# Two heads per transposing instruction and per set-aside copy in an attention and expert kernel, the last pair moved by copies, and a new order

## The chip, the cores and the metric

One core of one Trainium2 chip runs the whole program. The metric is device microseconds (us) of one execution; a time is the median of several. The core has five engines that this text calls by short names: PE (TensorE, matmuls), DVE (VectorE), ACT (ScalarE), POOL (GpSimd) and SP (SyncE, which here only issues DMAs). Each engine works through its own list of instructions in the order in which the program wrote them, and stops at an instruction whose inputs are not there yet.

## The reference

```python
q, k, v: (8, 8, 576, 64) float32            # batch, heads, sequence, head size
q_rot, k_rot = rotate(q), rotate(k)         # x1*cos - x2*sin, x1*sin + x2*cos
scores = matmul(q_rot, k_rot^T) / 8         # then minus the row maximum
attn = exp(scores) / (sum(exp(scores)) + 1e-9)
x = matmul(attn, v)                         # back to (8, 576, 512): heads side by side
for b in range(8):                          # routing and experts, one batch at a time
    score = x[b] @ w_gate
    top = the 128 tokens with the largest score
    y = relu(x[b, top] @ w1) @ w2           # w1 512x1024, w2 1024x512
    out[b] = x[b];  out[b, top] += sigmoid(score[top])[:, None] * y
```

## The kernel before, in words

Two heads of one batch make a pair; there are 32 pairs, four to a batch (`n_pairs`, `NP`). A pair goes through these steps, written by the functions named.

- `load` brings the pair's k, q and v from HBM. There is one buffer each for k and q (`k_in`, `q_in`), two for v (`vt`); half of v is copied once more to the other half of the partitions (L476, ACT or POOL).
- `rotate` makes the rotated k and q in two parts each, high and low, so that three matmuls of reduced precision give a float32 product. For every pair but the first this is POOL work: a product with the tables of cosines (L504), a sum (L510, and L514 for the last 64 places of q), and the difference from the rounded value (L520). ACT does the rounding (L519). For the first pair DVE does POOL's part, in pieces.
- `attend` does nine units of 128 rows: units 0 to 7 are four blocks of 128 positions for two heads, unit 8 holds the last 64 positions of both heads. `units` writes the matmuls of a unit, or of the two heads' units of a block together (L570: the groups qh kh, qh kl, ql kh). `softmax` then has DVE take the row minimum of the negated scores into SBUF (L591) and ACT the exponential and its sum (L599), into `pab` (two buffers, each with room for both heads of a block) or `pr` (unit 8).
- `turn` transposes a unit's 128x576 probabilities in 32x32 blocks by one DVE instruction (L622) into the tile `pt` and sets one half of the result aside by a copy of 128x288 (L628, ACT or POOL). `move` then exchanges halves between groups of 32 partitions by four DMAs on SP's queue (L654): two out of place, then two from the set-aside copy, which wait for the first two. This happens twice per pair: side 0 (`c` = 0) has units 0 to 3, side 1 has units 4, 5, 8, 6 and 7. For side 1 of the last pair the exchange is done by copies of 32x288 instead (L639, ACT or POOL), four per unit.
- `value` multiplies the transposed probabilities with v (L681, 36 instructions for a side, 72 passes in the trace), `rows_out` turns the result back (L734) and scales it by the reciprocal sums (L749 on ACT or L753 on DVE) into the rows of x; `half_done` stores them.
- After the fourth pair of a batch, `route` finds the 128 largest scores, `chosen` computes their indices (L896 is its last matmul), gathers those rows from HBM by an indirect DMA that POOL issues (L912), and `experts_of` transposes them (L930), does the two matrix products (L958, 192 instructions of the first and of the second each, over the eight batches) and scatters the result (L997, another indirect DMA of POOL). The tile `xe` is one buffer: a gather waits for the scatter of the batch before. The expert weights are loaded, rounded (L1022, ACT) and their low parts made (L1024, POOL, 16 instructions) beside the first pairs.

The order of all this is not the order in which it is written. Every step is entered with `op(engines, fn, key, after, ...)`: the engines that may do it with an assumed time for each, a due time `key` and the steps it must follow. `Order.run` then plays a small planner: at each moment it gives each free engine the waiting step with the smallest due time, whose inputs are ready by the assumed times, and where a step may go to one of two engines it goes to the one free first. The due times come from the dictionary `KEY` and a small random shift per pair drawn from `SEEDS`. When PE would be idle the planner adds a matmul that nobody reads (L367), if PE's recent busy share in its model is below `KEY["warm"]`. What is sent to the chip is then the list of instructions per engine in that order, with semaphores where one instruction reads or overwrites the data of another. The list `after` itself is read by the planner alone:

```python
o = op({"DVE": (675, 760)}, turns, key, exps[u] + area[c].before)
...
for _, _, o, e in order.run():
    o.fn(e) if len(o.engines) > 1 else o.fn()
```

Of the kernel before, what the change touches and what calls it, by code (L numbers as in the profile page):

```python
# [23 lines left out]
KEY = dict(warm=0.86, warm0=20000, warm1=1000000, dummy=430, dcols=256, ahead=15000, lag=16000, rem=400, value=17500, rows=5250, load=30500, rotate=173549, half=2500,
           gate=10237, route=21900, count=23781, select=5425, turn=24609, step=11400, count_=24062, select_=3000, turn_=98437, step_=10820, last_step=4750, kstep=2700, hold=3,
           vcopy=6000, lift=range(9), lifted=688, patience=900, over=450, near=-900, swap=9750, vsplit=9, vstep=2250, recip=7500, pool_lo=1, esplit=1, t_most=4, ring="SP", vring="SP", wring="SP", issue=250, svc0=800, svc1=200, svck=2101, svcq=2251, svcv=1501, first_moves=True, over_dma=750, patience_dma=1150)


SEEDS = (65, 53, 848, 188, 64, 106, 182, 56, 412, 765, 334, 840, 49, 811, 920, 630, 707, 350, 158, 580, 649, 829, 598,
         159, 606, 89, 919, 466, 149, 808, 916, 981, 466)  # L30
# [14 lines left out]
class Order:  # L45
# [4 lines left out]
    SEM = 45.0  # L50
    BLOCK, FETCH = 256, 3900.0
    WINDOW, FALL, RISE = 3413.0, 0.58, 0.88
    LANDED, FLYING = 500.0, 8


    TURN = {(a, b): t for t, froms, tos in (
# [222 lines left out]
def attention_moe_kernel(ctx: ExitStack, tc: tile.TileContext, q, k, v, gate, w1, w2, rope, outs, shape, cap):  # L279
# [51 lines left out]
    def act(n, more=0.0):  # L331
        return (65 + 0.833 * n + more, 165 + 0.833 * n + more)
# [120 lines left out]
    def at(pi, part):  # L453
        return PAIR * (pi + part)
# [34 lines left out]
    def rotate(pi):  # L489

        uses, got = loaded[pi]
        first = pi == 0
        key, base = at(pi, 0) - KEY["rotate"], at(pi, 0) - KEY["ahead"]
        if first:
            key = base = at(pi, 0) - 100000
        kh, kl, qh, ql = (r.next() for r in (khs, kls, qhs, qls))
        wait = list(last_first) if pi == 1 else []
        e = nc.vector if first else nc.gpsimd
        time = (lambda n: {"DVE": dve(n)}) if first else (lambda n: {"POOL": pool(n)})
        parts = {}  # L500

        def part(use, sum_use, sum_, tab, hu, lu, c0, c1, got, more=0):
            x, n = use.tile, c1 - c0
            m = op(time(2 * n), lambda: e.tensor_tensor(  # L504
                x[:, :, c0:c1], x[:, :, c0:c1], tab[:, :, c0:c1], op=ALU.mult), key + more, got)
            edge = name == "q" and c1 == S

            def add():
                m1 = MAIN if edge else c1
                e.tensor_tensor(sum_[:, c0:m1], x[:, 0, c0:m1], x[:, 1, c0:m1], op=ALU.add)  # L510
                for h in range(2) if edge else ():
                    hp = slice(64 * h, 64 * h + 64)
                    a, b = (x[hp, i, MAIN:S].rearrange("p (a j) -> p a j", j=32) for i in range(2))
                    e.tensor_tensor(striped(sum_)[hp, :, h], a, b, op=ALU.add)  # L514

            y = op(time(n) if not edge else {"DVE": dve(n, 1, 200.0)} if first else {"POOL": pool(MAIN, 540.0)}, add, key + more, [m] + sum_use.before)
            d1 = KW if edge else c1
            n = d1 - c0
            c = op({"ACT": act(n)}, lambda: nc.scalar.copy(hu.tile[:, c0:d1], sum_[:, c0:d1]), base + more, [y] + hu.before)  # L519
            d = op(time(n), lambda: e.tensor_tensor(  # L520
                lu.tile[:, c0:d1], sum_[:, c0:d1], hu.tile[:, c0:d1].bitcast(F32), op=ALU.subtract), base + more + 3000 * first, [c] + lu.before)
            use.by(m, y), sum_use.by(y, c, d), hu.by(c, d), lu.by(d)
            if first:
                last_first.append(y)
# [21 lines left out]
    def attend(pi):  # L546
# [61 lines left out]
        ready = lambda c: pts[c][:, area[c].tile:area[c].tile + 2 * (4 + c) * L]  # L608
        apart = lambda c: pts[c][:, side_[c].tile:side_[c].tile + (4 + c) * L]

        def turn(u, key):

            c = 1 if u == 8 else u // 4
            src, to = (pr.tile, 2) if u == 8 else (pab[u // 2].tile[:, u % 2 * S:u % 2 * S + S], (2 + c) * (u % 2) + u // 2 % 2)
            one = ready(c)[:, (1 + c) * to * L:(1 + c) * to * L + L]
            away = L if c else 4 * L
            two = bass.AP(tensor=one.tensor, offset=one.offset + away, ap=one.ap)

            def turns():
                into = one.rearrange("p (m o j) -> p m o j", o=1, j=32)  # L620
                into = bass.AP(tensor=into.tensor, offset=into.offset, ap=[*into.ap[:2], [away, 2], [1, 32]])
                nc.vector.transpose(into, src.rearrange("p (m w j) -> p m w j", w=2, j=32))  # L622

            o = op({"DVE": (675, 760)}, turns, key, exps[u] + area[c].before)
            (pr if u == 8 else pab[u // 2]).by(o)
# [8 lines left out]
            for g in (0, 2):
                e, o_ = slice(32 * g, 32 * g + 32), slice(32 * g + 32, 32 * g + 64)
                needs = [o, y]
                for out, in_ in ((two[e], one[o_]), (one[o_], apart(c)[e, to * L:to * L + L])):
                    needs = [op({"ACT": act(L, 30), "POOL": pool_copy(L)},
                                lambda e, out=out, in_=in_: (nc.gpsimd.tensor_copy if e == "POOL" else nc.scalar.copy)(out, in_),  # L639
                                key, needs)]  # L640
                    area[c].by(*needs), side_[c].by(*needs), moved[c].extend(needs)
# [510 lines left out]
```

## Time and profile before

| what | value |
| --- | --- |
| median of 3 runs | 584.03 us (583.14 to 585.76) |
| the profiled execution, its own time | 578.55 us |
| its span, first to last instruction | 576.5 us |
| PE busy, of which matmuls that nobody reads (L367) | 534.2 us, 51.9 us |
| DVE, ACT, POOL busy | 494.2, 478.2, 452.1 us |
| moved by DMA | 108.67 MB, mean 189 GB/s |
[...]

The profile is one execution, taken by the hardware profiler. Busy times are of the engine named; matmuls overlap, and their ends are modelled, so a busy PE is not PE at its peak. A row of instructions gives busy time, mean duration of one in ns, and how long the engine stood idle just before and what ended that. Durations of neighbours overlap at their ends: the spacing from start to start is shorter than a duration, and it is read from rows that merge several instructions.

### The profile page before, as it was taken

To read this page: it belongs to the slowest core of one execution; us is meant where nothing else is said; L and a number is where in the kernel's file an instruction comes from. 1 tells how busy PE (TensorE), PEld (TensorE's weight loads), DVE (VectorE), ACT (ScalarE), POOL (GpSimd) and SP (SyncE) were. 2 spreads that over 40 slices of the span, in tenths; PEclk is the share of its full clock that TensorE was granted. 3 is DMA by queue.
4 is the path that set the end of the run, shared out by engine and by line. 5 is a ranking of instruction groups with operands and counts; after the bars stand their busy time and mean duration, and the time that the engine had idled before them with its cause. 6 is when DMAs were issued, how large, how long until landed. Compare 5 with 4: busy or idle time off the path is not lost.

```text
span 576.5 us, 19632 instructions
## 1 busy us (share of the span) xinstructions
PE 534.2 (93%) x7558; PEld 443.7 (77%) x7558; DVE 494.2 (86%) x1249; ACT 478.2 (83%) x1307; POOL 452.1 (78%) x489
## 2 busy tenths in 40 slices
PE   2799999999999899989999999986999899999996
PEld 1587787788788688878788877765888787888885
DVE  7887899999999899988999979994999898989331
ACT  4788899999997999889998979785898998979521
POOL 2989999999998987969897998857899688825310
PEclk9989999999999999999999999997999999999999
DMA  7477887888676866676777687764776768555210
GB/s 238 136 215 223 238 240 214 244 221 240 197 225 189 227 175 194 198 234 192 198 224 197 185 213 177 191 195 131 219 198 193 227 178 214 156 131 157 63 38 18
DMA packets 56957, 108.67 MB, mean 189 GB/s; under 512 B 7072, under 2 KB 37664, under 8 KB 56864
## 3 DMA queue, kind: packets, MB, share of 16 engines
q1 hardware_dynamic: 54768, 102.58, 63.4%
q0 software_dynamic: 1280, 4.20, 2.4%
q8 instruction: 59, 0.97, 0.7%
q10 hardware_dynamic: 816, 0.66, 0.4%
q14 instruction: 34, 0.28, 0.2%
HBM read 54.14 MB, written 11.53 MB: 114 GB/s over the span
## 4 chain that ended last, share of the span: by engine, by line
PE 31%; ACT 19%; DMA 14%; POOL 14%; issue 11%; DVE 9%; SPq 1%; POOLq 0%; DVEq 0%; ACTq 0%
PE ps L681 9%; PE ps L570 9%; ACT pab L599 8%; PE ps L958 7%; DMA out_dram<-xe,idx 5%; DVE pab L591 3%; POOL q_in L504 3%; DVE pt L622 3%; DMA pt<-pt 3%; DMA k_in<-k_dram 3%; ACT pt L628 3%; DMA xe<-out_dram,idx 3%; PE ps L734 2%; POOL k_in L504 2%; ACT vt L476 2%
## 5 line engine op out<-in xcount | busy, mean ns | idle before, releaser
L599 ACT ACTIVATE pab<-pab,nm 128x576 f32<-128x576 f32 x256 | 197.1, 773 | 19.8 <-DVE pab L591 18.4
L622 DVE STREAM_TRANSPOSE pt<-pab 128x576 f32<-128x576 f32 x256 | 189.5, 761 | 17.4 <-ACT pab L599 15.9
L591 DVE TENSOR_SCALAR_CACHE_REDUCE pab<-ps 128x576 f32<-128x576 f32 x256 | 181.0, 745 | 22.8 <-PE ps L570 22.5
L681 PE MATMUL ps<-pt,vt 64*64 64x128 f32 (+1 forms) x4608 | 158.7, 286 | 2.5 <-ACT gp L751 1.8
L681 PEld LDWEIGHTS ps<-pt,vt 64*64 64x64 f32 x4608 | 140.8, 133 | 17.0 <-issue 6.5
L570 PE MATMUL ps<-kh,qh 64*128 64x288 f32 (+1 forms) x576 | 89.3, 352 | 13.7 <-ACT qh L519 10.2
L628 ACT COPY pt<-pt 128x288 f32<-128x288 f32 x220 | 87.9, 431 | 13.8 <-DVE pt L622 8.6
L504 POOL TENSOR_TENSOR k_in<-k_in,tabs 128x1152 f32<-128x1152 f32 x31 | 82.7, 2666 | 16.5 <-DMA k_in<-k_dram 15.9
L570 PEld LDWEIGHTS ps<-kh,qh 64*128 64x128 f32 (+1 forms) x576 | 51.2, 190 | 47.5 <-issue 12.8
L504 POOL TENSOR_TENSOR q_in<-q_in,tabs 128x1152 f32<-128x1152 f32 x31 | 82.8, 2669 | 3.4 <-DMA q_in<-q_dram 3.0
L570 PE MATMUL ps<-kh,ql 64*128 64x288 f32 (+1 forms) x576 | 71.3, 299 | 3.9 <-POOL ql L520 2.0
L570 PE MATMUL ps<-kl,qh 64*128 64x288 f32 (+1 forms) x576 | 70.7, 296 | 0.0
L570 PEld LDWEIGHTS ps<-kh,ql 64*128 64x128 f32 (+1 forms) x576 | 53.8, 190 | 4.7 <-POOL ql L520 2.5
L958 PE MATMUL ps<-w,xt 128*128 128x512 f32 x192 | 54.4, 413 | 0.0
L570 PEld LDWEIGHTS ps<-kl,qh 64*128 64x128 f32 (+1 forms) x576 | 53.9, 191 | 0.0
L734 PE MATMUL ps<-turner,ot 128*128 128x136 f32 x320 | 50.0, 287 | 3.6 <-ACT ot L356 3.0
L958 PE MATMUL ps<-w,ht 128*128 128x512 f32 x192 | 52.3, 409 | 0.0
L367 PE MATMUL ps<-tabs,turner 128*128 128x256 f32 x190 | 51.9, 398 | 0.0
L734 PEld LDWEIGHTS ps<-turner,ot 128*128 128x128 f32 x320 | 43.1, 189 | 10.5 <-ACT ot L356 4.8
L520 POOL TENSOR_TENSOR ql<-q_sum,qh 128x640 fp32r<-128x640 f32 x31 | 48.4, 1560 | 2.0 <-ACT qh L519 2.0
L599 ACT ACTIVATION_READ_ACCUMULATOR pab<-pab,nm 128x1 f32 x256 | 49.0, 191 | 0.0
L520 POOL TENSOR_TENSOR kl<-k_sum,kh 128x576 fp32r<-128x576 f32 x31 | 44.1, 1423 | 3.2 <-ACT kh L519 2.5
(110 smaller groups left out, 775.7 us busy)
## 6 DMA issues: line engine op xcount, KB each, us to landing
pt<-pt SPq DMA_DIRECT2D x124, 180.0 KB
pt<-pt SPq DMA_DIRECT2D x128, 144.0 KB
k_in<-k_dram SPq DMA_DIRECT2D x31, 576.0 KB
q_in<-q_dram SPq DMA_DIRECT2D x31, 576.0 KB
vt<-v_dram SPq DMA_DIRECT2D x32, 288.0 KB
out_dram<-x SPq DMA_DIRECT2D x16, 512.0 KB
xe<-w_dram SPq DMA_DIRECT2D x8, 256.0 KB
h<-w_dram SPq DMA_DIRECT2D x8, 256.0 KB
```

Of the source, the lines that this page charges most:

```text
L367: nc.tensor.matmul(bank_of(b)[:, 0:KEY["dcols"]], ident, tabs[:, 0, 0:KEY["dcols"]], start=True, stop=True)
L476: (nc.gpsimd.tensor_copy if e == "POOL" else nc.scalar.copy)(use.tile[mine, 1], use.tile[there, 0])
L504: m = op(time(2 * n), lambda: e.tensor_tensor(x[:, :, c0:c1], x[:, :, c0:c1], tab[:, :, c0:c1], op=ALU.mult), key + more, got)
L520: d = op(time(n), lambda: e.tensor_tensor(lu.tile[:, c0:d1], sum_[:, c0:d1], hu.tile[:, c0:d1].bitcast(F32), op=ALU.subtract), base + more ...
L570: nc.tensor.matmul(bank_of(bs[i])[:, n, 0:HALF], lt, rt, start=start, stop=stop)
L591: nc.vector.tensor_scalar(halves, bank_of(b)[:, :, 0:HALF], -1.0, None, op0=ALU.mult, op1=ALU.min, accum_out=nm.tile[:, u:u + 1])
L599: lambda: nc.scalar.activation(halves, halves if lift else bank_of(b)[:, :, 0:HALF], AF.Exp, bias=nm.tile[:, u:u + 1], scale=-1.0 if lift ...
L622: nc.vector.transpose(into, src.rearrange("p (m w j) -> p m w j", w=2, j=32))
L628: (nc.gpsimd.tensor_copy if e == "POOL" else nc.scalar.copy)(apart(c)[:, to * L:to * L + L], two)
L681: nc.tensor.matmul(bank_of(acc)[64 * h:64 * h + 64, g, c0:c0 + 32 * n], vt.tile[gp_, h ^ g, (m - 1) % 2 * NT + (m - 1) // 2 if m else 2 * ...
L734: nc.tensor.matmul(bank_of(b)[:, W * i:W * i + W], ot.tile[:, i * P:i * P + P], turner, start=True, stop=True)
L958: nc.tensor.matmul(bank_of(bank), lhs.tile[:, a, c * P:c * P + P], w[w_][:, c, fs], start=(c == 0 and i == 0), stop=(c == n - 1 and i == 2))
```

## The change

Four things are changed in the text of the kernel.

1. `turn` takes the two heads' units of a block together: one DVE transpose of 128x1152 instead of two of 128x576, and one set-aside copy of 128x2x288 instead of two of 128x288. Unit 8 stays as it is. Both wait for both heads' exponentials.
2. In the last pair, side 0 too is exchanged by copies of 32x288 (16 of them) instead of four DMAs.
3. The list `last_first`, which the planner puts before the rotation of the second pair, holds the first pair's low parts (`d`) beside its sums (`y`).
4. The numbers in `KEY`, the list `SEEDS` and the planner's assumed landing time of a DMA (`LANDED`, 500 to 1250) are others, and so is the order of instructions on every engine.

```diff
-KEY = dict(warm=0.86, ..., rows=5250, load=30500, rotate=173549, half=2500,
+KEY = dict(warm=0.82, ..., rows=3750, load=27500, rotate=216936, half=6250,
...
-SEEDS = (65, 53, 848, ...
+SEEDS = (902, 121, 623, ...
...
-    LANDED, FLYING = 500.0, 8
+    LANDED, FLYING = 1250.0, 8
...
             if first:
-                last_first.append(y)
+                last_first.extend((y, d))
...
-        def turn(u, key):
+        def turn(us, key):
...
+            n, used = len(us), pr if us[0] == 8 else pab[us[0] // 2]
+            before = sum((exps[u] for u in us), [])
             def turns():
-                into = one.rearrange("p (m o j) -> p m o j", o=1, j=32)
-                into = bass.AP(tensor=into.tensor, offset=into.offset, ap=[*into.ap[:2], [away, 2], [1, 32]])
-                nc.vector.transpose(into, src.rearrange("p (m w j) -> p m w j", w=2, j=32))
+                into = view(one, 0, [next_, n], [32, NB // 2], [away, 2], [1, 32])
+                nc.vector.transpose(into, used.tile[:, 0:n * S].rearrange("p (h m w j) -> p h m w j", h=n, w=2, j=32))
-            o = op({"DVE": (675, 760)}, turns, key, exps[u] + area[c].before)
+            o = op({"DVE": (75 + 600 * n, 160 + 600 * n)}, turns, key, before + area[c].before)
...
-                (nc.gpsimd.tensor_copy if e == "POOL" else nc.scalar.copy)(apart(c)[:, to * L:to * L + L], two)
+                out = view(apart(c), to * L, [(2 + c) * L, n], [1, L])
+                (nc.gpsimd.tensor_copy if e == "POOL" else nc.scalar.copy)(out, view(one, away, [next_, n], [1, L]))
...
-            if not c or pi < n_pairs - 1:
+            if pi < n_pairs - 1:
                 return [o, y]
+            for i in range(n):
...
-            if c and pi == n_pairs - 1:
+            if pi == n_pairs - 1:
                 return
...
-            turns = [turn(u, at(pi, 0) + UNITS.index(u) * step + KEY["swap"]) for u in mine]
+            turns = [turn(us, at(pi, 0) + UNITS.index(us[-1]) * step + KEY["swap"]) for us in STARTS if us[0] in mine]
```

Three places of the new order follow. Lines after 591 have shifted by up to 5: L622 is now L623, L628 L630, L639 L644, L681 L686, L734 L739, L896 L901, L912 L917, L930 L935, L997 L1002, L1024 L1029.

POOL, from the first low part of q of the second rotated pair on (`ql_85<-q_sum`, L520), before: the rotation of the third pair with the weight parts (`w`) between.

```order
L520 TENSOR_TENSOR ql_85<-q_sum_78,qh_83 128x640
L1024 TENSOR_TENSOR w_1_120<-h_109,w_0_119 128x512
L510 TENSOR_TENSOR q_sum_78<-q_in_75 128x512
L514 TENSOR_TENSOR q_sum_78<-q_in_75 64x2x32 x2
L1024 TENSOR_TENSOR w_1_120<-xe_110,w_0_119 128x512
L520 TENSOR_TENSOR kl_82<-k_sum_77,kh_80 128x576
L504 TENSOR_TENSOR k_in_76<-k_in_76,tabs 128x1152
L1024 TENSOR_TENSOR w_1_120<-h_109,w_0_119 128x512
L510 TENSOR_TENSOR k_sum_77<-k_in_76 128x576
L504 TENSOR_TENSOR q_in_75<-q_in_75,tabs 128x1152
L1024 TENSOR_TENSOR w_1_120<-xe_110,w_0_119 128x512
L520 TENSOR_TENSOR ql_86<-q_sum_78,qh_84 128x640
```

The same stretch of POOL now, from the same low part to that of the next pair.

```order
L520 TENSOR_TENSOR ql_85<-q_sum_78,qh_83 128x640
L504 TENSOR_TENSOR k_in_76<-k_in_76,tabs 128x1152
L504 TENSOR_TENSOR q_in_75<-q_in_75,tabs 128x1152
L510 TENSOR_TENSOR k_sum_77<-k_in_76 128x576
L510 TENSOR_TENSOR q_sum_78<-q_in_75 128x512
L514 TENSOR_TENSOR q_sum_78<-q_in_75 64x2x32 x2
L1029 TENSOR_TENSOR w_1_120<-h_109,w_0_119 128x512
L1029 TENSOR_TENSOR w_1_120<-xe_110,w_0_119 128x512
L520 TENSOR_TENSOR ql_86<-q_sum_78,qh_84 128x640
```

Weight parts have moved behind the rotations: counted over POOL's list, 11 of the 16 stood ahead of the fifth pair's `ql` and 7 stand there now.

POOL between the scatter of batch 3 (`out_dram<-xe`) and the gather of batch 4 (`xe<-out_dram`), before:

```order
L997 DMA out_dram<-xe_110,idx_114 576x512
L476 COPY vt_87<-vt_87 64x576
L628 COPY pt_92<-pt_92 128x288 x2
L716 COPY sums_99<-sums_99 32x1 x4
L911 CAST idx_113<-gg_117 128x1
L912 DMA xe_110<-out_dram,idx_113 128x512
```

and now:

```order
L1002 DMA out_dram<-xe_110,idx_114 576x512
L476 COPY vt_87<-vt_87 64x576
L630 COPY pt_92<-pt_92 128x2x288
L504 TENSOR_TENSOR q_in_75<-q_in_75,tabs 128x1152
L504 TENSOR_TENSOR k_in_76<-k_in_76,tabs 128x1152
L916 CAST idx_113<-gg_117 128x1
L917 DMA xe_110<-out_dram,idx_113 128x512
```

Two rotation products now stand between them. For batches 1 to 5 the count of such products there goes from 1, 0, 0, 0, 0 to 2, 1, 2, 2, 1.

PE at the same place: the last rows ahead of the transposes of the gathered rows (L930), before:

```order
L734 MATMUL ps<-turner,ot_94 128x136 x2
L367 MATMUL ps<-tabs,turner 128x256
L570 MATMUL ps<-kh_80,qh_84 128x288 x4
L570 MATMUL ps<-kl_82,qh_84 128x288 x4
L570 MATMUL ps<-kh_80,ql_86 128x288 x4
L681 MATMUL ps<-pt_93,vt_88 64x160 x36
L930 MATMUL ps<-turner,xe_110 128x128 x4
```

and now, from the same L681 (now L686) on:

```order
L686 MATMUL ps<-pt_93,vt_88 64x160 x36
L570 MATMUL ps<-kh_80,qh_84 128x288 x2
L570 MATMUL ps<-kl_82,qh_84 128x288 x2
L570 MATMUL ps<-kh_80,ql_86 128x288 x2
L570 MATMUL ps<-kh_80,qh_84 128x288 x4
L570 MATMUL ps<-kl_82,qh_84 128x288 x4
L570 MATMUL ps<-kh_80,ql_86 128x288 x4
L739 MATMUL ps<-turner,ot_95 128x136 x3
L367 MATMUL ps<-tabs,turner 128x256
L570 MATMUL ps<-kh_80,qh_84 128x288 x4
L570 MATMUL ps<-kl_82,qh_84 128x288 x4
L570 MATMUL ps<-kh_80,ql_86 128x288 x4
L935 MATMUL ps<-turner,xe_110 128x128 x4
```

Three score groups of PE that stood behind the transposes of the gathered rows now stand ahead of them.

## Rows read from the trace of the kernel before

**Rows 1.** The page: span, and busy time of the engines with instruction counts.

```profile
span 576.5 us, 19632 instructions
PE 534.2 (93%) x7558; PEld 443.7 (77%) x7558; DVE 494.2 (86%) x1249; ACT 478.2 (83%) x1307; POOL 452.1 (78%) x489
```

**Rows 2.** The page: the chain that ended last, shares by engine and by line.

```profile
PE 31%; ACT 19%; DMA 14%; POOL 14%; issue 11%; DVE 9%; SPq 1%; POOLq 0%; DVEq 0%; ACTq 0%
PE ps L681 9%; PE ps L570 9%; ACT pab L599 8%; PE ps L958 7%; DMA out_dram<-xe,idx 5%; DVE pab L591 3%; POOL q_in L504 3%; DVE pt L622 3%; DMA pt<-pt 3%; DMA k_in<-k_dram 3%; ACT pt L628 3%; DMA xe<-out_dram,idx 3%; PE ps L734 2%; POOL k_in L504 2%; ACT vt L476 2%
```

**Rows 3.** Windows: length, busy PE PEld DVE ACT POOL, TensorE clock, DMA share, GB/s.

```profile
32.00:96.00 64.00, 61.34 (x847) 50.31 (x843) 54.25 (x137) 56.78 (x149) 61.28 (x46) 1.00 0.83 234
96.00:160.00 64.00, 61.65 (x967) 51.68 (x962) 60.52 (x154) 62.82 (x173) 60.42 (x59) 1.00 0.78 223
160.00:384.00 224.00, 216.34 (x3218) 179.82 (x3214) 207.71 (x521) 199.25 (x559) 191.59 (x206) 1.00 0.73 203
392.00:397.00 5.00, 3.45 (x19) 2.84 (x20) 0.56 (x1) 1.25 (x3) 5.00 (x4) 0.50 0.53 127
```

**Rows 4.** Groups by line: busy us, mean ns of one, idle before and releasers.

```profile
L628 ACT COPY pt<-pt 128x288 f32<-128x288 f32 x220 | 87.9, 431 | 13.8 <-DVE pt L622 8.6 <-DMA pt<-pt 4.2
...
L504 POOL TENSOR_TENSOR k_in<-k_in,tabs 128x1152 f32<-128x1152 f32 x31 | 82.7, 2666 | 16.5 <-DMA k_in<-k_dram 15.9
...
L367 PE MATMUL ps<-tabs,turner 128*128 128x256 f32 x190 | 51.9, 398 | 0.0
...
L519 ACT CAST kh<-k_sum 128x576 fp32r<-128x576 f32 x31 | 20.9, 675 | 1.5 <-POOL k_sum L510 1.3
...
L1024 POOL TENSOR_TENSOR w<-h,w 128x512 fp32r<-128x512 f32 x8 | 10.3, 1287 | 0.9 <-ACT w L1022 0.9
```

**Rows 5.** Timeline: start, length, engine, line, operation, count [idle before <-releaser]; paces.

```profile
20.76 2.75 DVE L622 STREAM_TRANSPOSE pt<-pab 128x576 f32<-128x576 f32 x4
...
250.30 0.75 ACT L628 COPY pt<-pt 128x288 f32<-128x288 f32 x2
...
542.90 1.31 ACT L749 ACTIVATE x<-ps,rs 128x64 f32<-128x64 f32 x6 [0.50 <-PE ps L734]
```

**Rows 6.** Timeline of the start, the first pair's rotation on DVE.

```profile
7.95 0.75 DVE L504 TENSOR_TENSOR k_in<-k_in,tabs 128x576 f32<-128x576 f32 x1
...
10.07 1.08 DVE L504 TENSOR_TENSOR q_in<-q_in,tabs 128x896 f32<-128x896 f32 x1
...
12.78 2.64 POOL L504 TENSOR_TENSOR k_in<-k_in,tabs 128x1152 f32<-128x1152 f32 x1 [10.35 <-DMA k_in<-k_dram]
...
13.61 2.35 DVE L520 TENSOR_TENSOR ql<-q_sum,qh 128x512 fp32r<-128x512 f32 x1
...
16.02 0.85 PE L570 MATMUL ps<-kh,ql 64*128 64x288 f32 x4 [1.88 <-DVE ql L520]
```

**Rows 7.** Timeline of POOL and PE between the scatter of batch 3 and the gather of 4.

```profile
377.45 1.06 POOL L997 DMA_INDIRECT out_dram<-xe,idx  x1 [0.28 <-POOL q_sum L514]
...
382.66 0.54 PE L570 MATMUL ps<-kh,qh 64*128 64x288 f32 x4
...
383.65 2.68 PE L681 MATMUL ps<-pt,vt 64*64 64x160 f32 x72
...
385.76 0.61 POOL L716 COPY sums<-sums 32x1 f32<-32x1 f32 x3 [5.39 <-DMA out_dram<-xe,idx]
...
387.28 1.06 POOL L912 DMA_INDIRECT xe<-out_dram,idx  x1 [0.66 <-POOL idx L911]
...
393.55 1.11 PE L930 MATMUL ps<-turner,xe 128*128 128x128 f32 x4 [7.22 <-DMA xe<-out_dram,idx]
```

**Rows 8.** Waits over the whole span: us in total, times, longest.

```profile
PE ps L930 <- DMA xe<-out_dram,idx: 13.1, 4, 7.2
```

**Rows 9.** Timeline of the tail.

```profile
532.51 0.76 ACT L599 ACTIVATE pab<-pab,nm 128x576 f32<-128x576 f32 x1
...
536.88 5.10 PE L681 MATMUL ps<-pt,vt 64*64 64x160 f32 x144
```

More of the change, by code (lines that the diff above doesn't have):

```diff
@@ L21 @@
 EPS = 1e-9
[L24 to L30, printed above, removed]
+KEY = dict(warm=0.82, warm0=20000, warm1=1000000, dummy=430, dcols=256, ahead=15000, lag=16000, rem=400, value=17500, rows=3750, load=27500, rotate=216936, half=6250,
+           gate=10237, route=21900, count=23781, select=6175, turn=24609, step=11400, count_=24062, select_=2250, turn_=110741, step_=10820, last_step=3250, kstep=2700, hold=3,
+           vcopy=6000, lift=range(9), lifted=688, patience=1400, over=450, near=-1500, swap=8531, vsplit=9, vstep=3000, recip=7500, pool_lo=1, esplit=1, t_most=4, ring="SP", vring="SP", wring="SP", issue=250, svc0=725, svc1=176, svck=1901, svcq=1901, svcv=1051, first_moves=True, over_dma=1050, patience_dma=150)
+SEEDS = (902, 121, 623, 210, 771, 805, 573, 723, 500, 960, 372, 593, 589, 679, 211, 34, 983, 784, 189, 971, 133, 26,
+         282, 141, 142, 18, 547, 283, 773, 586, 274, 378, 685)
 NOISE = 300.0
@@ L609, in attend @@
         apart = lambda c: pts[c][:, side_[c].tile:side_[c].tile + (4 + c) * L]
-        def turn(u, key):
-            c = 1 if u == 8 else u // 4
-            src, to = (pr.tile, 2) if u == 8 else (pab[u // 2].tile[:, u % 2 * S:u % 2 * S + S], (2 + c) * (u % 2) + u // 2 % 2)
+        def turn(us, key):
+            c = 1 if us[0] == 8 else us[0] // 4
+            n, used = len(us), pr if us[0] == 8 else pab[us[0] // 2]
+            to = 2 if us[0] == 8 else us[0] // 2 % 2
+            away, next_ = L if c else 4 * L, (1 + c) * (2 + c) * L
@@ L615, in turn @@
             one = ready(c)[:, (1 + c) * to * L:(1 + c) * to * L + L]
-            away = L if c else 4 * L
-            two = bass.AP(tensor=one.tensor, offset=one.offset + away, ap=one.ap)
+            view = lambda x, off, *dims: bass.AP(tensor=x.tensor, offset=x.offset + off, ap=[x.ap[0], *dims])
+            before = sum((exps[u] for u in us), [])
             def turns():
-                into = one.rearrange("p (m o j) -> p m o j", o=1, j=32)
-                into = bass.AP(tensor=into.tensor, offset=into.offset, ap=[*into.ap[:2], [away, 2], [1, 32]])
-                nc.vector.transpose(into, src.rearrange("p (m w j) -> p m w j", w=2, j=32))
@@ L624, in turn @@
-            o = op({"DVE": (675, 760)}, turns, key, exps[u] + area[c].before)
-            (pr if u == 8 else pab[u // 2]).by(o)
+                into = view(one, 0, [next_, n], [32, NB // 2], [away, 2], [1, 32])
+                nc.vector.transpose(into, used.tile[:, 0:n * S].rearrange("p (h m w j) -> p h m w j", h=n, w=2, j=32))
+            o = op({"DVE": (75 + 600 * n, 160 + 600 * n)}, turns, key, before + area[c].before)
+            used.by(o)
             def aside_of(e):
-                (nc.gpsimd.tensor_copy if e == "POOL" else nc.scalar.copy)(apart(c)[:, to * L:to * L + L], two)
@@ L630, in turn @@
-            y = op({"ACT": act(L, 30), "POOL": pool_copy(L)}, aside_of, key, [o] + side_[c].before)
+                out = view(apart(c), to * L, [(2 + c) * L, n], [1, L])
+                (nc.gpsimd.tensor_copy if e == "POOL" else nc.scalar.copy)(out, view(one, away, [next_, n], [1, L]))
+            y = op({"ACT": act(n * L, 30), "POOL": pool_copy(n * L)}, aside_of, key, [o] + side_[c].before)
             area[c].by(o, y), side_[c].by(y)
-            if not c or pi < n_pairs - 1:
+            if pi < n_pairs - 1:
@@ L633, in turn @@
                 return [o, y]
[L634 to L641, printed above, removed]
+            for i in range(n):
+                one_, two_ = (view(one, x + i * next_, [1, L]) for x in (0, away))
+                aside_ = view(apart(c), to * L + i * (2 + c) * L, [1, L])
+                for g in (0, 2):
+                    e, o_ = slice(32 * g, 32 * g + 32), slice(32 * g + 32, 32 * g + 64)
+                    needs = [o, y]
+                    for out, in_ in ((two_[e], one_[o_]), (one_[o_], aside_[e])):
+                        needs = [op({"ACT": act(L, 30), "POOL": pool_copy(L)},
+                                    lambda e, out=out, in_=in_: (nc.gpsimd.tensor_copy if e == "POOL" else nc.scalar.copy)(out, in_),
+                                    key, needs)]
+                        area[c].by(*needs), side_[c].by(*needs), moved[c].extend(needs)
```

## Prediction

> **What bounds the kernel now.** I read the busy shares first. PE is busy 534.2 of 576.5 us, but 51.9 of that are matmuls that nobody reads [rows 1, 4]; the 482.3 that count are 84%, beside DVE's 86%, ACT's 83% and POOL's 78%. No engine stands out, so a single saved instruction is not worth its length. The chain that ended last says how the end is shared: PE 31%, ACT 19%, DMA and POOL 14% each, DVE 9% [rows 2]. The windows then show that the limit changes along the program. From 32 to 96 us POOL has 61.28 of 64 us and ACT is idle for 7.2; from 96 to 160 ACT has 62.82 of 64; later PE is nearly full and POOL has slack, 191.59 of 224 [rows 3]. So the opening is set by POOL's rotations, the next stretch by ACT, and the rest by PE with its stops. The largest stop is PE's wait for the gathered rows, 13.1 us in four places [rows 8], 7.22 of it at one [rows 7], after which the granted clock is 0.50, the lower of the two levels, for some 5 us [rows 3].
>
> This is one profiled execution of 578.55 us, 5.5 below the median of 584.03. I make the sum against 578.55 and add it to the median unchanged. About 0.5%, 2.9 us, is what a measurement can tell from no change.
>
> **(a) Fewer, larger instructions.** 256 transposes of 128x576 become 128 of twice the size; the 32 of unit 8 stay. Four in a row take 2.75 us, and as the first or last lasts about 0.76 the spacing is 0.66 [rows 5]. A second head costs 576 elements: DVE took 0.75 for 576 and 1.08 for 896 of another operation, 1.03 ns each [rows 6], so 0.59. A pair goes from 1.33 to 1.25: 0.08 x 128 = 10.2 us less. In both orders I count what DVE takes over: 9 products of x (half of a 576's 0.75, 0.4) and 17 small copies (0.2), +7.0. DVE: -3.2.
> ACT's two copies of 288 take 0.75, one alone 0.43 [rows 4, 5], spacing 0.32; one of 576 lasts 0.675 by the rounding of that size [rows 4], spacing about 0.56. ACT goes from 220 singles to 27 and 106 doubles: -61.8 + 59.4 = -2.4. It gives away 36 scalings of x at 0.2 [rows 5], 7 copies of v at about 0.67 and 17 small ones at 0.2, and takes 20 sums at 0.2 and 7 moves at 0.43: -15.3 + 7.0 = -8.3. ACT: -10.7. POOL's set-aside copies, at the same prices with a double taken as 0.75, give -63 x 0.43 + 22 x 0.75 = -10.6; with 7 v copies, 9 moves more and 20 sums fewer, -6.
> Weighted by the chain's shares, 19% of 10.7, 9% of 3.2 and 14% of 6 make **-3**. Bounds: 0 (the slower of two partners always waited for anyway) to -10.7 (ACT the limit throughout).
> [...]
>
> **(b) Opening.** The new POOL order puts 7 instead of 11 weight parts of 1.29 us [rows 4] ahead of the fifth pair's low part: the rotations, POOL's limit there, come up to 5.2 us earlier. ACT, next in line, has 7.2 us to give until 96, but only 1.2 in the 64 after that [rows 3]. The four parts come back where POOL has about 3.6 of 64 idle, a thin cover; if it goes, the gain goes. I take **-3**, between 0 and -5.2.
>
> **(c) Gathers.** POOL issued the scatter at 377.45, did some copies, stood 5.39 us until the scatter landed, and issued the gather at 387.28; PE got its rows at 393.55 after 7.22 idle [rows 7]. The change moves two things. PE has more work ahead of L930: a score group is 0.99 (382.66 to 383.65) [rows 7]; with the reads of x and unused matmuls counted in both orders, batches 1 to 5 get 4.6, 2.4, 0.2, 3.9 and 1.0 us, 12.1 in all. Against it, seven more products of 2.67 [rows 4] stand between scatter and gather, and everything behind them on POOL (the index, the gather) and then PE waits. But the first of each could run in the stop, as the copies do: two products beside a stop of 5.39 delay by one. If cover is met by idle at each place, the best is -9, and -11 with the slow clock; if all seven delay, 18.7 - 12.1 = +6.6. I take **-5**: five of seven hide, two cost 5.3 against the 9, which would leave -4, and part of the slow clock adds a unit.
>
> **(d) Tail.** After the last exponential at 532.51 all 144 passes for v of the last pair run together from 536.88, 5.10 us [rows 9]. Side 0, now without DMAs, is ready earlier in PE's order, so one side's 2.68 [rows 7] can go ahead of that. Its 16 moves of 0.43 are beside other work on two engines; uncovered they push the end by 3.4. Taken **-2**, bounds -2.7 and +3.4. Four DMAs leave SP's queue, where nothing stands behind them that is urgent.
>
> **(e) First low part.** The list `after` is the planner's alone, and POOL's first product has the same inputs to wait for in both programs. Only DVE moves: `ql` goes ahead of one row minimum, 0.7 earlier. In the row `ql` started at 13.61 beside POOL's product, took 2.35, and ended 0.54 after that product's end (15.42) [rows 6]; from 12.9 it would still be behind the product that began at 12.78. So **0**; bounds -1.9 (PE's idle before the group that reads it [rows 6]) and +0.7, the row minimum now behind it.
> [...]
>
> **(f) Coarser units.** The transpose waits for both heads and its copy for all 1152: from last exponential to copy done a side takes 0.76 + 0.43 = 1.19 now and 1.35 + 0.68 = 2.03 then, +0.84. The two lines hold 3% each of the chain, 34.6 us, or 29 sides of 64 [rows 2]: at most 24.4. A later side costs PE only where it has no other real work, idle (42.3) or unused (51.9) for 16% of the span [rows 1, 4]: **+4**, bounds 0 and 24.4.
>
> Sum: -3 - 3 - 5 - 2 + 0 + 4 = -9, so 569.55 for such an execution and **575.0 as the median**.
>
> **The rivals.** *Engine work and opening worth nothing* (no engine alone is the limit; partners set the pace): -9 + 6 = -3, 581.0. For it: four shares between 78 and 86%. Against it: the windows from 32 to 160.
> *Gathers later instead of covered*: (c) at +6.6, 11.6 worse, +2.6, 586.6. For it: the products stand ahead of the gather on POOL. Against it: POOL's stop hides part.
> *More of each gain*: about (a) -7, (b) -4, (c) -8, (d) -2.6, (e) -1, (f) +1: 562.4. The saved copies would have to count in the ACT stretch and most of PE's stops vanish.
> *The change does not do what it says*: in (e) it sets no wait on the chip; that is in the sum at 0.
> **Slower**: (f) at its full price, +11.4, 595.4. The place is the side's end, from last exponential to product with v, with the pace set by that loop and not by free engines. It is slower from (f) of 17 on, that is if 20 of the 29 sides pass their 0.84 on. For it: ACT's copies already stand 8.6 us waiting for the transposes [rows 4], so the loop is tight. Against it: a buffer of two blocks, and unused matmuls to give way.
>
> **How the numbers follow.** Forecast 0.43 (its own range 567 to 581), engine work worth nothing 0.16, gathers later 0.15, more of each 0.11, slower 0.15. Faster by over 0.5% (below 581.1): the forecast, the high gain and 0.10 of the second case, 0.64. Within: 0.06 of the second and 0.10 of the gathers' case, 0.16. Slower (above 587): 0.05 and 0.15, 0.20. The range 564 to 588 leaves out about half of the high gain and most of the slow case, some 0.19.
>
> **What would show it.** Right: a double transpose near 1.35 us long and a copy near 0.68; POOL's rotations ending earlier and ACT fuller from 32 to 96; waits of L935 on the gather well under 13.1 and no window at 0.50; the last 72 passes after the last exponential alone. Wrong: a double of twice the single's time; POOL's product after the stop and the gather over 3 us later; `ql` at 0.7 us; PE idle on transposes or copies where there was none, or more unused matmuls, which would be (f).

## The result and the profile after

The changed kernel is slower: 587.55 us median of 21 runs beside 582.12 of 21 runs of the kernel before, a ratio of 1.0083 (95% interval 1.0055 to 1.0111), so some 4.8 us. The ratios here and below leave out runs more than 1.5% above the fastest of their kernel, so they can differ from the quotient of the medians, which is 1.0093 here. The forecast was 575.0, faster. The profiled execution of the changed kernel took 588.62 us, above its median, and that of before 578.55, below its own: the two traces lie 10 us apart, twice what the medians do, and that has to be kept in mind where their rows are set side by side.

The page: span, busy engines, the chain by engine and by line [rows 1, 2].

```profile
span 586.9 us, 19313 instructions
PE 540.2 (92%) x7548; PEld 443.4 (76%) x7548; DVE 492.3 (84%) x1148; ACT 469.5 (80%) x1186; POOL 447.4 (76%) x444
...
PE 30%; DMA 18%; ACT 17%; POOL 16%; DVE 9%; issue 8%; SPq 1%; POOLq 0%; DVEq 0%; ACTq 0%
PE ps L686 9%; PE ps L570 9%; PE ps L963 7%; ACT pab L599 7%; DMA pt<-pt 6%; POOL q_in L504 4%; DVE pt L623 4%; DMA vt<-v_dram 3%; ACT pt L630 3%; POOL k_in L504 3%; DVE pab L591 3%; PE ps L739 3%; DMA q_in<-q_dram 3%; POOL kl L520 2%; DMA h<-w_dram 2%
```

All three other engines have less to do than before, DVE by 1.9, ACT by 8.7 and POOL by 4.7 us (worked out ahead: 3.2, 10.7 and 6), and the span is longer. (PEld, the loading of weights, runs beside PE: their 443.4 and 540.2 us lie in a span of 586.9.) In the chain the exchange (`DMA pt<-pt`) has gone from 3% to 6% and loads of v have come in with 3%. PE was idle 42.3 us before and is 46.7 now, and it was also busy 6.0 us longer, though it has ten fewer of the matmuls that nobody reads. The passes for v take most of it (before first):

```profile
L681 PE MATMUL ps<-pt,vt 64*64 64x128 f32 (+1 forms) x4608 | 158.7, 286 | 2.5 <-ACT gp L751 1.8
...
L686 PE MATMUL ps<-pt,vt 64*64 64x128 f32 (+1 forms) x4608 | 163.1, 291 | 7.3 <-DMA pt<-pt 5.1
```

The groups of the larger instructions, and of the matmuls that nobody reads [rows 4]:

```profile
L623 DVE STREAM_TRANSPOSE pt<-pab 128x1152 f32<-128x1152 f32 x128 | 174.7, 1370 | 28.7 <-ACT pab L599 26.2 <-DMA k_in<-k_dram 1.9
...
L367 PE MATMUL ps<-tabs,turner 128*128 128x256 f32 x180 | 50.8, 400 | 1.5 <-DVE pab L591 1.2 <-ACT gp L756 0.3
...
L630 ACT COPY pt<-pt 128x576 f32<-128x576 f32 x106 | 70.9, 672 | 26.8 <-DMA pt<-pt 14.1 <-DVE pt L623 7.8 <-DVE pab L591 3.4
```

The sizes are as worked out: 1.37 us a double transpose, 0.67 a double copy. What changed is the idle time ahead of them. Waits, before first (us in total, times, longest):

```profile
DVE pt L622 <- ACT pab L599: 15.9, 29, 2.0
...
POOL pt L628 <- DVE pt L622: 9.1, 11, 2.3
...
ACT pt L628 <- DVE pt L622: 8.6, 15, 2.1
...
ACT pt L628 <- DMA pt<-pt: 4.2, 3, 2.7
...
PE ps L570 <- DVE pab L591: 0.7, 2, 0.4
```

and after, with the waits of PE that answer to [rows 8] or are new:

```profile
DVE pt L623 <- ACT pab L599: 26.2, 27, 3.1
...
ACT pt L630 <- DMA pt<-pt: 14.5, 9, 3.9
...
PE ps L935 <- DMA xe<-out_dram,idx: 7.0, 3, 5.2
...
PE ps L686 <- DMA pt<-pt: 5.1, 6, 2.0
PE ps L570 <- DVE pab L591: 4.5, 5, 2.2
```

PE's wait for gathered rows has halved, from 13.1 to 7.0, as forecast. Two others have taken its place: passes for v on the exchange, and scores on DVE's row minima. One of the latter shows how: a load of v lands 8 us after its issue, a copy of v stands in ACT's list ahead of exponentials, a double transpose of DVE waits for these, the row minima stand behind it in DVE's list, and PE comes to rest behind them (timeline of the changed kernel):

```profile
314.07 0.58 SPq L469 DMA_DIRECT2D vt<-v_dram  x1
...
322.09 1.35 ACT L476 COPY vt<-vt 64x576 f32<-64x576 f32 x2 [2.35 <-DMA vt<-v_dram]
...
325.14 1.38 DVE L623 STREAM_TRANSPOSE pt<-pab 128x1152 f32<-128x1152 f32 x1 [3.13 <-ACT pab L599]
...
327.90 0.53 PE L570 MATMUL ps<-kh,qh 64*128 64x288 f32 x4 [2.19 <-DVE pab L591]
```

After this stop the granted clock is at 0.50, the lower level, where it was 1.00 in the kernel before (320 to 352 us). The window from 330 to 335 (length, busy PE PEld DVE ACT POOL, clock, DMA share, GB/s):

```profile
330.00:335.00 5.00, 5.00 (x50) 4.46 (x54) 4.98 (x14) 4.14 (x10) 1.25 (x2) 0.50 1.01 295
```

From 320 to 352 us 284 passes for v took 10.66 us at a mean clock of 0.89, where 304 took 10.00 at 1.00 in the same window before; so part of PE's longer busy time is the clock.

Where along the program the time goes is read from POOL's scatters, one per batch. Before (the first, the sixth and the last):

```profile
181.32 1.06 POOL L997 DMA_INDIRECT out_dram<-xe,idx  x1
...
507.79 1.06 POOL L997 DMA_INDIRECT out_dram<-xe,idx  x1 [4.56 <-DVE xe L993]
...
572.27 1.01 POOL L997 DMA_INDIRECT out_dram<-q_in,idx  x1 [13.04 <-DVE q_in L993]
```

After (with the fourth, which answers to 377.45 in [rows 7]):

```profile
185.95 1.06 POOL L1002 DMA_INDIRECT out_dram<-xe,idx  x1 [0.58 <-DVE xe L998]
...
381.99 1.06 POOL L1002 DMA_INDIRECT out_dram<-xe,idx  x1 [0.16 <-issue]
...
515.89 1.05 POOL L1002 DMA_INDIRECT out_dram<-xe,idx  x1 [2.95 <-DVE xe L998]
...
582.67 1.00 POOL L1002 DMA_INDIRECT out_dram<-q_in,idx  x1 [14.35 <-DVE q_in L998]
```

In these two traces 4.6 us are lost by the first scatter, none more net by the fourth, 3.6 from there to the sixth, and 2.3 in the tail.

### The profile page after: what moved, and what is told of

Same layout as the page of the kernel before. It is cut to its first block, busy times and chain, and to the rows that moved or that the text cites. A ratio compares the mean times of both kernels' runs of the same rounds, so it can differ in the third digit from the quotient of the medians.

```text
span 586.9 us, 19313 instructions
## 1 busy us (share of the span) xinstructions
PE 540.2 (92%) x7548; PEld 443.4 (76%) x7548; DVE 492.3 (84%) x1148; ACT 469.5 (80%) x1186; POOL 447.4 (76%) x444
## 4 chain that ended last, share of the span: by engine, by line
PE 30%; DMA 18%; ACT 17%; POOL 16%; DVE 9%; issue 8%; SPq 1%; POOLq 0%; DVEq 0%; ACTq 0%
PE ps L686 9%; PE ps L570 9%; PE ps L963 7%; ACT pab L599 7%; DMA pt<-pt 6%; POOL q_in L504 4%; DVE pt L623 4%; DMA vt<-v_dram 3%; ACT pt L630 3%; POOL k_in L504 3%; DVE pab L591 3%; PE ps L739 3%; DMA q_in<-q_dram 3%; POOL kl L520 2%; DMA h<-w_dram 2%
## 5 line engine op out<-in xcount | busy, mean ns | idle before, releaser
L623 DVE STREAM_TRANSPOSE pt<-pab 128x1152 f32<-128x1152 f32 x128 | 174.7, 1370 | 28.7 <-ACT pab L599 26.2
L686 PE MATMUL ps<-pt,vt 64*64 64x128 f32 (+1 forms) x4608 | 163.1, 291 | 7.3 <-DMA pt<-pt 5.1
L686 PEld LDWEIGHTS ps<-pt,vt 64*64 64x64 f32 x4608 | 144.6, 136 | 22.2 <-issue 6.0
L630 ACT COPY pt<-pt 128x576 f32<-128x576 f32 (+1 forms) x133 | 80.6, 622 | 27.2 <-DMA pt<-pt 14.5
L504 POOL TENSOR_TENSOR k_in<-k_in,tabs 128x1152 f32<-128x1152 f32 x31 | 82.9, 2675 | 17.2 <-DMA k_in<-k_dram 16.9
L739 PE MATMUL ps<-turner,ot 128*128 128x136 f32 x320 | 52.4, 295 | 4.2 <-ACT ot L356 3.4
L520 POOL TENSOR_TENSOR ql<-q_sum,qh 128x640 fp32r<-128x640 f32 x31 | 48.5, 1564 | 9.0 <-ACT qh L519 8.8
L739 PEld LDWEIGHTS ps<-turner,ot 128*128 128x128 f32 x320 | 43.0, 192 | 12.9 <-ACT ot L356 6.1
L520 POOL TENSOR_TENSOR kl<-k_sum,kh 128x576 fp32r<-128x576 f32 x31 | 44.1, 1423 | 3.9 <-ACT kh L519 3.4
```

The lines of the kernel that those rows point to most:

```text
L504: m = op(time(2 * n), lambda: e.tensor_tensor(x[:, :, c0:c1], x[:, :, c0:c1], tab[:, :, c0:c1], op=ALU.mult), key + more, got)
L520: d = op(time(n), lambda: e.tensor_tensor(lu.tile[:, c0:d1], sum_[:, c0:d1], hu.tile[:, c0:d1].bitcast(F32), op=ALU.subtract), base + more ...
L623: nc.vector.transpose(into, used.tile[:, 0:n * S].rearrange("p (h m w j) -> p h m w j", h=n, w=2, j=32))
L686: nc.tensor.matmul(bank_of(acc)[64 * h:64 * h + 64, g, c0:c0 + 32 * n], vt.tile[gp_, h ^ g, (m - 1) % 2 * NT + (m - 1) // 2 if m else 2 * ...
L739: nc.tensor.matmul(bank_of(b)[:, W * i:W * i + W], ot.tile[:, i * P:i * P + P], turner, start=True, stop=True)
```

## The experiments

Theory U: the larger units cost, because a side is ready later. Theory D: the new order costs, whatever the units. Ratios are to the kernel before, with their 95% intervals. In the fixed-order kernels every engine's list keeps its sequence, and only what is named differs.

**Units and numbers.** Split the units in the changed order; merge them in the old order; exchange the planner's numbers.

```diff
# e1_split: the changed kernel
-                into = view(one, 0, [next_, n], [32, NB // 2], [away, 2], [1, 32])
...
+                for i in range(n):
+                    into = view(one, i * next_, [32, NB // 2], [away, 2], [1, 32])
...
# e2_merge: the kernel before
+                state[0] += 1
+                if state[0] < n:
+                    return
...
# e3_numbers: before with the new KEY, SEEDS, LANDED; e4_oldnum: the reverse
```

> The changed kernel with its order kept on every engine, but each double transpose issued as two of 128x576 in a row and each double set-aside copy as two of 128x288. Theory U (the larger units cost: a side is ready 0.8 us later): 3 to 5 us faster than the changed kernel, so 1.000 to 1.003 of before. Theory D (the new order costs, whatever the units): as the changed kernel, 1.008, or a little slower, up to 1.012, since DVE gets some 10 us of work back.

> The kernel before with its order kept, but the two transposes of a block issued as one at the place of the second, and the two set-aside copies likewise (the last pair's side 1 stays single). Theory U: 3 to 6 us slower than before, 1.005 to 1.010, with more wait of transposes on exponentials and of copies and passes on the exchange. Theory D: no slower, 0.994 to 1.001, because DVE and ACT lose work.

> The kernel before, single units, with the changed kernel's numbers (KEY, SEEDS, LANDED); the planner makes a new order from them. Theory U: near 1.000, at most 1.004. Theory D: 1.008 or more. A third view, that any order not fitted to its units is worse: 1.01 to 1.03 here and in the next run alike.

> The changed kernel, double units, with the numbers of before. Theory U: 1.006 to 1.012 of before, as the changed kernel or worse. Theory D: 0.995 to 1.002. Third view: 1.01 to 1.03.

Measured: e1_split 1.0163 (1.0119 to 1.0207), e2_merge 1.0058 (1.0020 to 1.0096), e3_numbers 1.0062 (1.0017 to 1.0108), e4_oldnum 1.0200 (1.0158 to 1.0242). Neither theory holds alone. Merging costs in the old order, as U says; but splitting costs too in the new order, which U denies. Two of these figures are others by the medians of all runs: e2_merge is 1.0023 and e3_numbers 1.0125. Of these kernels, each fixed order does best with the units it was made for.

**Buffers in the changed order.** Are the new waits on the exchange (theory X) and on loads (theory L) what costs? Rings hand out one tile more, while the planner counts the old number, so that the order stays.

```diff
-        use = Use(self.tiles[self.at], self.users[self.at])
+        i = self.at % len(self.users)
+        use = Use(self.tiles[self.at % len(self.tiles)], self.users[i])
...
# a_aside2, a_all
-    AREAS, SIDES = (2, 2), 1
+    AREAS, SIDES = (2, 2), 2
```

> The changed kernel, its order kept on every engine, with two buffers in turn for the set-aside halves of each side instead of one (to make room, the low parts of the second expert weight share space, so three quarters of them are replaced by others). Theory X (the exchange: ACT's set-aside copy stands behind the previous pair's transfers, 14.5 us): that wait goes to under 5 us and the time falls by 4 to 6 us, to 0.998 to 1.002 of before. Theory L (late loads): 1.006 to 1.009. Theory N (no buffer matters, the sequence on the engines does): 1.008.

> The changed kernel, order kept, with three buffers in turn for v instead of two (same room made). Theory L: SP no longer stands 19.4 us for PE with v, so transfers behind it start earlier, ACT's 8.6 us and the fall of the clock at 329 us go: 2 to 4 us faster than the changed kernel, 1.001 to 1.005. Theories X and N: 1.007 to 1.009.

> The changed kernel, order kept, with two buffers each for k and q instead of one (same room made). Theory L: SP no longer stands 39.7 us for POOL's sums, POOL's waits on q and k (9.6 and 6.5 us without the first) go, 2 to 4 us faster than the changed kernel, 1.001 to 1.005. X and N: 1.007 to 1.009.

> All three at once (room made by sharing the low parts of both expert weights). X and L together: 8 us or more faster than the changed kernel, 0.994 or less. X alone: as with the two set-aside buffers. N: 1.006 to 1.009.

Measured: a_aside2 1.0070 (1.0036 to 1.0104), a_v3 1.0135 (1.0069 to 1.0201), a_kq2 1.0118 (1.0059 to 1.0176), a_all 1.0080 (1.0037 to 1.0124). With a second set-aside buffer ACT's wait on the exchange is gone from the list of waits, and DVE's on exponentials has shrunk:

```profile
DVE pt L624 <- ACT pab L600: 18.0, 21, 3.8
ACT pt L631 <- DVE pt L624: 9.2, 15, 1.4
...
PE ps L687 <- DMA pt<-pt: 6.3, 8, 1.8
```

The time has hardly moved: by the ratios 0.8 us of the 14.5 that ACT had waited, with intervals that overlap; by the medians of all runs some 2. PE's own wait on the exchange stayed, 6.3 us beside 5.1. X as the main cause falls. For L, more room for loads bought nothing, but that tests it only in part: in a_kq2 POOL's wait on k fell from 16.9 to 11.3 us, its wait on q did not (10.2 beside 9.6).

**Merging where nothing has to wait its turn; the tail alone; a new draw.** In the old order 68 of 128 pairs of transposes and 63 pairs of copies are neighbours on their engine.

```diff
# e9_adj: before
+        if hasattr(o.fn, "who") and getattr(f, "who", None) == o.fn.who and f.mate is None and f.__name__ == o.fn.__name__:
+            if all(place_[id(x)] > place_[id(o)] for x in was.outs):
+                f.mate, o.fn.mate = "gone", "both"
...
# e10_tail: before
-            if not c or pi < n_pairs - 1:
+            if pi < n_pairs - 1:
# d_sA: the changed kernel, s_sA: the same numbers with single units
-SEEDS = (902, 121, 623, ...
+SEEDS = (464, ...
```

> The kernel before, order kept on every engine; only where the two transposes of a block stand next to each other on DVE (68 of 128) they are one instruction, and likewise the set-aside copies (63). Nothing waits behind another instruction. Theory A (fewer instructions are worth what the prediction's first term says, and only the order takes it away): 0.993 to 0.998. Theory U (the larger unit itself costs): 1.002 to 1.006, as half of the 1.0058 of all pairs merged.

> The kernel before, with side 0 of the last pair exchanged by copies too; its order changes only from the last pair on. By the prediction's tail term 0.995 to 0.998 (2 us). Rival: the sixteen copies push the last side's own copies and the gain is gone or turns: 1.000 to 1.004.

> The changed kernel with other random shifts (SEEDS drawn anew), all other numbers kept. If an order is a draw: anywhere from 1.005 to 1.03, and more than 0.4% away from 1.0083. If the changed kernel's numbers decide: 1.006 to 1.011.

> Single units with the same numbers and the same new shifts as the run before. If larger units cost: 0.5% or more below that run. If they gain: 0.5% or more above it. If the order decides: either way, with no common sign to the pairs so far (before and its numbers with double units 1.000 and 1.020, the changed numbers 1.006 and 1.008).

Measured: e9_adj 1.0060 (1.0023 to 1.0098), e10_tail 1.0048 (1.0006 to 1.0090), d_sA 1.0399 (1.0321 to 1.0476), s_sA 1.0173 (1.0109 to 1.0237). So even neighbours lose by being one instruction, and as much as all pairs merged. The tail by copies alone loses some 2.8 us. Its timeline:

```profile
508.68 1.06 POOL L997 DMA_INDIRECT out_dram<-xe,idx  x1 [4.40 <-DVE xe L993]
...
527.56 1.34 ACT L639 COPY pt<-pt 32x288 f32<-32x288 f32 x3
...
536.30 0.76 ACT L599 ACTIVATE pab<-pab,nm 128x576 f32<-128x576 f32 x1
...
541.38 2.68 PE L681 MATMUL ps<-pt,vt 64*64 64x160 f32 x72
...
576.13 1.01 POOL L997 DMA_INDIRECT out_dram<-q_in,idx  x1 [14.34 <-DVE q_in L993]
```

From the start of the last exponential to the end of the passes it now takes 7.76 us (536.30 to 544.06), where it was 9.47 before (532.51 to 541.98, [rows 9]): the 1.7 us that the forecast meant. But the last exponential itself starts 3.8 us later, while the sixth scatter was only 0.9 later: seven of these copies, 3.00 us together, stand on ACT between exponentials ahead of it, where one of 0.43 stood before. And the one new draw shows the size of chance, more than was expected: shifts alone move the changed kernel by 3%.

**Which half of the merge, the moved low part, and a control.**

```diff
# e9t_turns / e9c_copies: only one kind is merged
+        ... f.__name__ == o.fn.__name__ == "turns":
# e11_ql: before
+    sent.insert(j, sent.pop(i))
# b_none: before, tiles elsewhere in memory
```

> A control: the kernel before, every engine's list the same, only tiles moved in memory (the low parts of the second expert weight share space, so three quarters of them are replaced by others). Expected 0.998 to 1.002; if it is 1.004 or more, then part of what the other runs show is an offset of any recompiled kernel, and no cost of units or tail.

> Kernel before, order kept; only the 68 neighbouring pairs of transposes are one instruction, the set-aside copies stay single. If the late first transpose is what costs (DVE's wait on exponentials went from 15.9 to 28.1 us in the run with both): 1.003 to 1.007. If the copies cost: 0.998 to 1.001.

> Kernel before, order kept; only 63 neighbouring pairs of set-aside copies are one instruction, the transposes stay single. If the late transpose costs: 0.997 to 1.001. If the copies cost: 1.003 to 1.007.

> Kernel before, with one exchange on DVE alone: the first pair's low part of q goes ahead of the second row minimum, as in the changed kernel. By the prediction it starts near 12.9 us, is still held beside POOL's product, ends near 16.0, and the time is 0.999 to 1.001. Rival: it ends by 14 us and PE's wait of 1.9 us goes: 0.996 to 0.998.

Measured: b_none 1.0009 (0.9973 to 1.0046), e9t_turns 1.0059 (1.0019 to 1.0098), e9c_copies 0.9978 (0.9932 to 1.0023), e11_ql 1.0052 (1.0011 to 1.0093). The control is at no change, so the losses are not an offset of any other build. For the neighbouring pairs it is the transposes that cost (by the medians of all runs 1.0072, and 0.9992 for the copies). The waits of e9t_turns (its lines have shifted):

```profile
DVE pt L632 <- ACT pab L599: 29.8, 45, 2.1
ACT pt L646 <- DVE pt L632: 18.5, 23, 3.3
POOL pt L646 <- DVE pt L632: 13.3, 11, 2.1
```

DVE waits for exponentials 45 times instead of 29, and the copies wait for transposes 31.8 us on ACT and POOL together, where it was 17.7. DVE itself has less to do, 489.9 us beside 494.2. These waits are not yet the cause: with all pairs merged (e2_merge) DVE waits no more than before,

```profile
ACT pt L644 <- DVE pt L633: 17.4, 22, 2.5
DVE pt L633 <- ACT pab L599: 14.8, 21, 1.7
```

and only the copies wait longer, 29.4 us with POOL's 12.0; in e9c_copies, which costs nothing, the copies wait 25.5 us, and in the control 22.6. On which path the transposes lose the time is not shown. For e11_ql the ratio says slower, but the medians of all runs lie 0.3 us apart (580.75 and 580.47), so I take it as no gain, and leave the loss open. Its forecast missed what `ql` does: it started at 13.13, took 0.69 us and ended at 13.82 instead of near 16.0 (last section). PE's wait of 1.9 us for it is gone, but PE then waits 2.7 us for POOL's first `ql` and not 1.6.

**The same halves in the changed order.**

> The changed kernel, order kept; only the double transposes are issued as two of 128x576 in a row, the set-aside copies stay double. If the double transpose costs in any order: faster than the changed kernel, 1.001 to 1.006. If an order made for doubles is dragged by DVE's returned work: 1.010 to 1.016.

> The changed kernel, order kept; only the double set-aside copies are issued as two of 128x288 in a row. If, as in the order of before, double copies save: 1.010 to 1.014. If the copies are indifferent: 1.007 to 1.010.

Measured: e1t_split 1.0159 (1.0101 to 1.0216), e1c_split 1.0203 (1.0135 to 1.0271), the latter beyond what was expected. Splitting the transposes, which takes DVE's wait on exponentials back to the old figure,

```profile
DVE pt L624 <- ACT pab L599: 15.4, 17, 2.3
```

does not bring the time back. The line that names the wait is real, and yet taking the wait away gains nothing in this order. The copies have one sign in both orders: merged they cost nothing in the old one, 0.9978, and to split them in the new one loses 1.2%.

## Why the prediction was wrong

Point by point, by its own steps:

- **(a) and (f), fewer and coarser units.** Taken as -3 and +4, together +1. In the order of before the merge costs 1.0058, or 3.4 us of 582 (1.3 by the medians of all runs), and where it could be taken apart the transposes cost and the copies do not. That a coarser unit costs, as (f) says, came true. Either its size was too low by up to some 2 us, or the gain of (a) was not there; the copies alone give 0.9978, within no change. Weighting by the chain's shares credited DVE's saved time as a gain, and in e9t_turns DVE saved 4.3 us, waited 13.9 longer, and the kernel gained nothing.
- **(b) Opening.** Forecast -3. POOL's rotations did come earlier: of the pair that the count of 11 and 7 weight parts belongs to, the fifth that POOL rotates, `kl` begins at 81.38 instead of 87.14 and `ql` at 85.81 instead of 88.52. The time did not follow: the first scatter is 4.6 us later. In the window PE is busy for less, and its clock has fallen where it was 1.00 [rows 3]:

```profile
32.00:96.00 64.00, 59.06 (x817) 48.09 (x816) 55.41 (x123) 58.75 (x151) 60.08 (x46) 0.97 0.83 229
96.00:160.00 64.00, 60.91 (x908) 49.57 (x906) 56.40 (x133) 59.61 (x155) 60.27 (x51) 1.00 0.79 228
```

  ACT took up 2 us of its slack up to 96, as forecast. PE's 2.3 us less are no lost work: the matmuls that nobody reads fell by 4.7 (first two lines, before and after, 32 to 96; busy PE and PEld), and one block of scores more was begun by 96 (last two lines):

```profile
32.00:96.00 64.00, 21.02 (x80) 13.92 (x80) 1.00 0.83 234
...
32.00:96.00 64.00, 16.28 (x60) 10.22 (x61) 0.97 0.83 229
...
0.00:96.00 96.00, 33.83 (x288) 26.48 (x288) 0.98 0.75 217
...
0.00:96.00 96.00, 34.23 (x300) 26.66 (x300) 0.98 0.73 209
```

  By 160 this head start is gone: 494 score matmuls beside 498, and one side of passes for v fewer (1080 weight loads beside 1152). ACT, which was to be the next limit there, is busy 59.61 us instead of 62.82. So the step that failed is that rotations done earlier, on the one engine that was nearly full, were booked as time of the kernel. What took the head start back is not shown.
- **(c) Gathers.** Forecast -5, and PE's wait fell by 6.1. As a statement on that wait it was right in direction; the closeness is in part luck. In the eight kernels with the changed order the wait is 7.0 to 9.7 us, in the old order 9.5 to 14.6, but 6.9 in e2_merge, where nothing at the gathers was changed. The cover that the step counted on failed at its own example, batch 4: POOL again stood until the scatter had landed, and both products came behind that stop, not in it.

```profile
390.07 0.66 POOL L476 COPY vt<-vt 64x576 f32<-64x576 f32 x1 [7.02 <-DMA out_dram<-xe,idx]
...
394.07 2.66 POOL L504 TENSOR_TENSOR k_in<-k_in,tabs 128x1152 f32<-128x1152 f32 x1
...
397.13 1.09 POOL L917 DMA_INDIRECT xe<-out_dram,idx  x1 [0.27 <-POOL idx L916]
...
402.41 1.11 PE L935 MATMUL ps<-turner,xe 128*128 128x128 f32 x4 [5.20 <-DMA xe<-out_dram,idx]
```

  From scatter to gather it is 15.14 us there, 9.83 before [rows 7], and the clock was at 0.50 again from 402 to 406. As a term of the sum the step failed: in place of the 6.1 us came PE's waits on the exchange, 5.1, and on row minima, 4.5 beside 0.7, and PE's idle time rose by 4.4 in all.
- **(d) Tail.** Forecast -2, bounds -2.7 and +3.4; alone it costs 2.8 us. The 1.7 us behind the last exponential are real, and the sixteen copies, which were taken as covered, go with a delay of that exponential by about 3. The value was taken at the wrong end of its own bounds.
- **(e) First low part.** Forecast 0, and right in its place. In the changed kernel `ql` started at 12.96, 0.09 us after POOL's product, and ended at 16.04, nearly as before (15.96), both times 0.54 behind the end of that product (where DVE came first, in e11_ql, it ended at 13.82):

```profile
12.87 2.63 POOL L504 TENSOR_TENSOR k_in<-k_in,tabs 128x1152 f32<-128x1152 f32 x1 [10.44 <-DMA k_in<-k_dram]
12.96 3.08 DVE L520 TENSOR_TENSOR ql<-q_sum,qh 128x512 fp32r<-128x512 f32 x1
...
16.75 0.78 ACT L599 ACTIVATE pab<-pab,nm 128x576 f32<-128x576 f32 x1 [2.92 <-DVE pab L591]
```

  The row minimum now behind it made the second exponential 3.0 us later (16.75, 13.71 before), more than the bound of +0.7 allowed.

Measured one at a time in the old order, the merge and the tail make +6.2, and the whole change +4.8: these two with nothing gained by (b) and (c) would explain the result. Of the 13.8 us between the forecast of -9 and +4.8, (d) would then be 4.8, (a) and (f) 2.4, and the rest, 6.6, most of the -8 of (b) and (c), which did not come. That they add up so in the new order is not shown, and there the splits speak against it. What stays open is why splitting both kinds costs in the one order, as merging both costs in the other. For the transposes alone the opposite sign is not clear of noise: the intervals, 1.0101 to 1.0216 and 1.0055 to 1.0111, touch. What the runs do show is that each of the two orders was slowed or left alone by every edit tried on it, that the other kernel's numbers cost single units 0.6% and double units 1.2% (1.0200 beside 1.0083), and that new shifts alone cost single units 1.1% (1.0173 beside 1.0062) and double ones 3.1%. As I read it, each is a good draw for exactly its own instructions; no run shows this by itself. With the same numbers and shifts, double units were slower or equal in all three pairs (1.0200 beside 1, 1.0083 beside 1.0062, 1.0399 beside 1.0173; by the medians of all runs the second pair is 1.0093 beside 1.0125). The rival "slower" named a place that costs, but its (f) of 24 us was far too large: some 6, if (a) is left at -3. A sum of small losses at every place where an order fits its instructions was not among the cases.

No version ran that beats both kernels; merged copies alone, 0.9978, are not clear of no change.

## What to carry to other kernels

Before booking a saved or moved wait as time, ask which wait ends last once it is gone; here 6 us taken from one wait of PE came back as two others. An instruction that serves two producers is ready when the later one is: count how often its engine, and what stands behind it, already waits for that producer (DVE 29 times here) before counting the time it saves. And when the order of the work is itself fitted, hold it fixed to measure an edit, make a control that changes nothing, and do not expect an edit to show its gain in an order made for other instructions.

## What was not expected of the hardware

In these rows the lengths of VectorE's `ql` and of GpSimd's product, which run at the same time, go with which of the two starts first. In the run with `ql` moved alone, DVE came first, by 10 ns:

```profile
13.13 0.69 DVE L520 TENSOR_TENSOR ql<-q_sum,qh 128x512 fp32r<-128x512 f32 x1
13.14 3.20 POOL L504 TENSOR_TENSOR k_in<-k_in,tabs 128x1152 f32<-128x1152 f32 x1 [10.72 <-DVE pab L592]
```

The same `ql` took 2.35 us before, 3.08 in the changed kernel and 0.69 here, while POOL's product took 2.64, 2.63 and 3.20. In the first two the product had started first, by 0.83 and 0.09 us, and `ql` ended 0.54 us after it; here the product ended 2.52 us after `ql` and took 0.56 us longer than before. What makes the later one longer is not shown.
